# Retention and two MLPs on one core: when out-product operands are begun, which banks they fill, and where loads and weight conversions stand

## The chip, the core and the metric

The kernel runs on one core of a Trainium2 chip. TensorE (PE) multiplies matrices into PSUM banks of 128 x 512 fp32, VectorE (DVE), ScalarE (ACT) and GpSimd (POOL) work element by element, each on its own queue in order, and SyncE (SP) issues the DMAs. Times are device microseconds of one launch.

## The reference

```python
for t in range(S):                                  # 4 batches, 8 heads, 768 steps, head size 64
    state = gamma * state + outer(k[:, :, t], v[:, :, t])
    y[:, :, t] = scale * q[:, :, t] @ state
x = y as rows of 512                                # 3072 rows
h = np.maximum(x @ w_in, 0.0)                       # 512 x 2048
x = h * h @ w_out                                   # 2048 x 512
xn = x / np.sqrt(np.mean(x * x, axis=-1, keepdims=True) + 1e-06) * rms_g
g = xn @ w_gate                                     # 512 x 1536
out = (g * (1 / (1 + np.exp(-g))) * (xn @ w_val)) @ w_out2   # 1536 x 512
```

## The kernel before

**Numbers.** Every large product is made of three: an operand is cut into a high part (a cast to fp32r, by ACT) and a low part (source minus high, by DVE), and high x high, high x low and low x high are summed in a bank (`mm3`). The weights arrive as 64-bit floats. `convert` makes fp32 of them: one ACT operation (`magnitude`, L146) and two integer operations on DVE (L151, L152) per step of 128 x 512. A **tick** (`tick`) finishes step i-1, starts the magnitude of i+1 and converts i; `fetch` asks SP for the raw weight three steps ahead. W1 has 32 steps, W2 36. A finished W2 step is written back to DRAM (`finish2`, wq and wp); magnitudes have three buffers (tile f), so the magnitude of a tick takes the buffer whose write the tick before issued.

**Stages.** The tokens are six blocks of 512 (four chunks of 128, one of each batch). The recurrence is done by chunks: scores of queries and keys times a decay table (tile Pt, DVE), times values, plus queries times state. All but the first four chunks are done in **visits** between the products of the block before: `into_state` (keys times values), `values`, `scores` of the next chunk.

1. *Lead-in* (0 to 22.46 us): chunks 0 to 3, first weights.
2. *Block 0* and *block 1* (to about 258 us): `block1`. A step f is 12 products with w_in (`proj`, bank ph[f % 2]), Relu and square, and 12 products with w_out of the step before (`out1`, banks pa, pb). Block 0 converts W1; in block 1 `factory` combines pieces of w_out into seven operand tables per quarter (Winograd's form of a 2 x 2 product, P1 to P7).
3. Blocks 2, 3 as the *first pair*, 4, 5 as the *second*. *In-phase* (`in_phase`): steps f of two projections, t = 0, 1, Relu and square into tiles act. *Out-phase* (`out_phase`): 28 units of 12 products, seven products of four units each, with differences of act as operands. P2, P5 and P3 are summed in pr, P1, P6, P7 and P4 in ph; after four units the sum is copied (`take`, ACT) or added (`add`, DVE). `operand(n + ahead)` makes a whole operand: difference (DVE, L97), cast (ACT, L93), low part (DVE, L90). W2 is converted in both in-phases. The second in-phase also loads the sums of blocks 0 and 1 (yn) and their scales (rr) and prepares second-MLP operands from them (`prep_x`); the second out-phase makes its first weight units (`make_unit`).
4. *Second MLP* (from 657.39 us): three pairs of blocks, each of twelve turns of `pair`: seven products of 12, and 24 products with the last weight.

The norm (`rsqrt`) sums squares with a product against ones, then takes root, reciprocal and one Newton step in pieces that `background` calls one at a time.

**Order.** The program is written out by hand: on each queue the instructions stand as the Python code issues them, and each waits for its operands in that place.

Of the kernel before, what the change touches and what calls it, by code (L numbers as in the profile page):

```python
# [38 lines left out]
PREP_IN = 8  # L39

# [11 lines left out]
def retention_then_two_mlps(  # L52
# [85 lines left out]
    def fetch(i):  # L138
        if i < upto[0] and i not in loads:
            loads[i] = wp.tile([128, 512, 2], I32, tag="w", name="raw")  # L140
            nc.sync.dma_start(loads[i].rearrange("p n t -> p (n t)"), steps[i][2].bitcast(I32))
# [6 lines left out]
    def convert(i):  # L148
# [7 lines left out]
        fetch(i + 3)  # L156

    def tick(low_first=False):
# [5 lines left out]
        if i < upto[0]:  # L164
            magnitude(i)
            magnitude(i + 1)
# [8 lines left out]
    def more_steps(n):  # L175
        upto[0] = min(upto[0] + n, len(steps))
        for i in range(at[0], at[0] + 3):
            fetch(i)
# [27 lines left out]
    def proj(w, x, h):  # L206
        xh, xl = x[0], x[1]
        for k in range(KC):
            wc = slice(k * 128, (k + 1) * 128)
            mm3(h, w[:, 0, wc], w[:, 1, wc], xh[k], xl[k], k == 0, k == KC - 1)  # L210
# [38 lines left out]

    def rsqrt(js, sqs, last=False):  # L250
# [5 lines left out]
        m = tp.tile([128, n, 2 * C], F32, tag="y", name="m")  # L256
        for i in range(n):
            nc.vector.tensor_scalar(m[:, i], tots[0][i], 1.0 / DM, EPS, op0=ALU.mult, op1=ALU.add)
        r = tp.tile([128, n, 2 * C], F32, tag="y", name="rr")
# [9 lines left out]
        for i, j in enumerate(js):  # L269
            nc.sync.dma_start(rrs[j].rearrange("(a b) t -> a (b t)", a=2), r[0:128:D, i, :])  # L270
# [60 lines left out]
    NOUT = 7 * NQ  # L331
    prepared = {}

    def operand(n, pairs):
        if n >= NOUT or n in prepared:
            return
        k, q = divmod(n, NQ)
# [9 lines left out]
        prepared[n] = pairs(n)  # L347
        split(*prepared[n], {P2: x10, P1: x00, P5: x00, P6: x00, P7: x01, P3: x11, P4: x10}[k], nc.vector)

    def out_phase(s, pairs, ahead, y_tile, extra):  # L350
# [8 lines left out]

        for n in range(NOUT):  # L360
            k, q = divmod(n, NQ)
            acc = pr if k in (P2, P5, P3) else ph
            u = units(next_unit())
            xh, xl = prepared.pop(n)
            for m in range(2):
                mc = slice(m * 128, (m + 1) * 128)
                for c in range(2):
                    mm3(
                        acc[m], u[:, c, 0, mc], u[:, c, 1, mc], xh[:, c], xl[:, c],
                        k in (P2, P1, P5) and q == 0 and c == 0, q == NQ - 1 and c == 1, skip_group_check=True,  # L370
                    )
            unit_done()
            if q == NQ - 1:
# [8 lines left out]
            operand(n + ahead, pairs)  # L382
            extra(n, y)
        return y
# [165 lines left out]
    with tc.manual_schedule():  # L550
# [13 lines left out]
        def put(c, qq, k_, vv, kk, *more):  # L564
            nc.sync.dma_start(qq, qT[c])
            nc.sync.dma_start(k_, kT[c])
            for m in more:
                nc.sync.dma_start(*m)
            nc.sync.dma_start(vv, vn[c])
            chunk[c] = (qq, k_, vv, kk)  # L570

        def load(c):
            if c < NCH:
# [6 lines left out]
                for t, src in zip(chunk[c][2:], (vn, kn)):  # L580
                    nc.sync.dma_start(t, src[c])
# [11 lines left out]
        def stage(c, *more):  # L593

            t = [slot(f"stage{c}{i}") for i in range(2)]
            qq, k_ = (t[0][:, i, :].rearrange("p (a i) -> p a i", a=NP) for i in range(2))
            vv, kk = (t[1][:, i, :].rearrange("p (a h d) -> p a h d", a=NP, h=2) for i in range(2))
            put(c, qq, k_, vv, kk, *more)
# [79 lines left out]
        def visit(c, next_banks, with_sums):  # L678
            kv = into_state(c)
            if with_sums:  # L680
                sums([pr[0][:, 2 * C:]])
# [12 lines left out]
        stage(0, *((decays[:, h], dec[:, h]) for h in range(2)))  # L694
        for t, src in ((vdec_sb, vdec), (sdec_sb, sdec), (tri_sb, tri)):
            nc.scalar.dma_start(t, src)
        fetch(0)
        for c in range(1, CB):
            stage(c)
        fetch(1)  # L700
# [9 lines left out]
        keep_warm(WARM)  # L710
        nc.sync.dma_start(chunk[0][3], kn[0])
        fetch(2)
# [4 lines left out]
        cur = Operand(True)  # L717

        def early_values(c, bank):
            values(c, [bank.rearrange("p (a i) -> p a i", a=NP)])  # L720
            cur.put(columns_of(c), [bank.rearrange("p (a i) -> p a i", a=NP)])

        scores(0, pa, early=True)
        keep_warm(WARM // 2)
        magnitude(0)
        convert(0)
        scores(1, pb, early=True)
        early_values(0, pr[1])
        low0 = finish1(w1_keys[0], done.pop(0))
        decay_v(0, nc.scalar)  # L730
        scores(2, pa, early=True)
        low0()
        early_values(1, pr[0])
        scores(3, pb, early=True)
        early_values(2, ph[0])
        early_values(3, ph[1])
        magnitude(1)
        convert(1)
        magnitude(2)
        at[0] = 2  # L740
        for c in range(1, CB):
            nc.sync.dma_start(chunk[c][3], kn[c])
        nc.sync.dma_start(g_sb, rmsg)

        def first_states(f):

            for c, n in enumerate((0, 2, 6, 10)):
                if f == n:
                    take_state(c, into_state(c))
            if f == 0:  # L750
                load(CB + 1)
                load_q(CB + 1)
            if f == 1:
# [420 lines left out]
```

## Time and profile before

| | |
|---|---|
| median of 3 runs | 1219.46 us (1215.66 to 1223.73) |
| profiled execution | 1216.87 us, span 1215.0 us |
| busy: PE, PE weight loads | 1155.6 us (95%), 934.2 us (77%) |
| busy: DVE, ACT, POOL | 743.0 us (61%), 593.7 us (49%), 44.4 us (4%) |
| mean granted TensorE clock | 0.985 |
| DMA | 175.46 MB, 144 GB/s |

A busy PE is not a PE at its pace: a product of 512 columns is shown as about 392 ns, but the next one starts after 227 ns, so delays below that difference show nowhere as idle. A stage is therefore also read as its length against its number of products. "Idle before" is put down to what came last.

### The profile page before, as it was taken

The numbers are of one execution on the slowest core, as the hardware profiler recorded it, in microseconds if no ns is written. First come the engines' busy times: TensorE is split into PE (matmuls) and PEld (weight loads), VectorE is DVE, ScalarE is ACT, GpSimd is POOL, SyncE is SP. The second block draws the span as 40 slices with busy tenths as digits, with TensorE's granted clock in tenths as the row PEclk, the third lists the DMA queues.
The fourth block names the chain that finished last, engine by engine and source line by source line (L and its number), as shares of the span: only waits on it lengthen the run. The fifth ranks groups of instructions, "written<-read, shape, count | busy, mean of one in ns | idle before, by whom it ended". The sixth has DMA issues, their size and how long they took to land.

```text
span 1215.0 us, 15870 instructions
## 1 busy us (share of the span) xinstructions
PE 1155.6 (95%) x6070; PEld 934.2 (77%) x6070; DVE 743.0 (61%) x1090; ACT 593.7 (49%) x1071; POOL 44.4 (4%) x39
## 2 busy tenths in 40 slices
PE   7899999899999899799897899999999999999998
PEld 6688887678887688577675688888888888888887
DVE  5777346733525665444666777876777766777740
ACT  4788545355544336555245455443554443454431
POOL 0000121112110000000000000000000000000000
PEclk9899999999999999899999999999999999999999
DMA  9662436677893469983551031122111131211001
GB/s 356 232 224 83 139 122 231 220 258 271 259 338 126 170 208 342 344 283 121 181 182 67 30 96 53 44 90 88 54 56 35 44 121 62 70 35 44 27 1 70
DMA packets 74212, 175.46 MB, mean 144 GB/s; under 512 B 7948, under 2 KB 20632, under 8 KB 73880
## 3 DMA queue, kind: packets, MB, share of 16 engines
q1 hardware_dynamic: 73560, 174.24, 41.1%
q8 instruction: 48, 0.79, 0.3%
q10 hardware_dynamic: 576, 0.20, 0.1%
q14 instruction: 28, 0.23, 0.1%
HBM read 129.31 MB, written 45.10 MB: 144 GB/s over the span
## 4 chain that ended last, share of the span: by engine, by line
PE 77%; DVE 10%; ACT 7%; issue 3%; DMA 3%; SPq 0%; ACTq 0%; DVEq 0%
PE ph L181 13%; PE ph L182 12%; PE ph L183 12%; PE pr L181 7%; PE pr L182 7%; PE pr L183 7%; DVE act L97 2%; PE pa L181 2%; PE pa L182 2%; PE pa L183 2%; PE pb L181 2%; PE pb L183 2%; PE pb L182 2%; ACT o L93 2%; DMA wq<-f 1%
## 5 line engine op out<-in xcount | busy, mean ns | idle before, releaser
L181 PE MATMUL ph<-xop,ring 128*128 128x512 f32 x288 | 113.5, 394 | 6.0 <-DVE part L100 5.8
L182 PE MATMUL ph<-xop,ring 128*128 128x512 f32 x288 | 112.6, 391 | 0.0
L183 PE MATMUL ph<-xop,ring 128*128 128x512 f32 x288 | 112.6, 391 | 0.0
L181 PE MATMUL ph<-xh,w_i 128*128 128x512 f32 x256 | 102.0, 398 | 5.7 <-DVE Pt L626 5.0
L182 PE MATMUL ph<-xl,w_i 128*128 128x512 f32 x256 | 100.4, 392 | 0.2 <-DVE xl L90 0.2
L183 PE MATMUL ph<-xh,w_i 128*128 128x512 f32 x256 | 100.3, 392 | 0.0
L181 PE MATMUL pr<-xop,ring 128*128 128x512 f32 x216 | 85.0, 393 | 1.4 <-DVE part L100 1.3
L182 PE MATMUL pr<-xop,ring 128*128 128x512 f32 x216 | 84.8, 393 | 0.0
L183 PE MATMUL pr<-xop,ring 128*128 128x512 f32 x216 | 84.6, 392 | 0.0
L90 DVE TENSOR_TENSOR o<-act,o 128x1024 fp32r<-128x1024 f32 x38 | 45.9, 1223 | 52.8 <-ACT o L93 52.8
L90 DVE TENSOR_TENSOR ring<-q,ring 128x512 fp32r<-128x512 f32 x90 | 57.4, 686 | 32.0 <-ACT ring L93 32.0
L93 ACT CAST o<-act 128x1024 fp32r<-128x1024 f32 x38 | 39.1, 1049 | 63.0 <-DVE act L97 60.0
L181 PEld LDWEIGHTS ph<-xop,ring 128*128 128x128 f32 x288 | 54.4, 189 | 20.1 <-DVE part L100 6.2
L183 PEld LDWEIGHTS ph<-xop,ring 128*128 128x128 f32 x288 | 54.4, 189 | 11.4
L182 PEld LDWEIGHTS ph<-xop,ring 128*128 128x128 f32 x288 | 54.4, 189 | 11.1
L181 PEld LDWEIGHTS ph<-xh,w_i 128*128 128x128 f32 x256 | 48.4, 189 | 18.4 <-DVE Pt L626 6.7
L327 ACT ACTIVATE act<-ph 128x512 f32<-128x512 f32 x64 | 38.0, 594 | 49.0 <-PE ph L183 48.5
L181 PE MATMUL ph<-xh,ring 128*128 128x512 f32 x128 | 51.0, 398 | 10.0 <-ACT act L327 10.0
L146 ACT ACTIVATE f<-raw 128x512 f32<-128x512 f32 x68 | 45.4, 669 | 29.9 <-DMA wq<-f 16.0
L480 ACT ACTIVATE t<-part 128x512 f32<-128x512 f32 x54 | 34.2, 633 | 45.9 <-DVE part L100 44.6
L183 PEld LDWEIGHTS ph<-xh,w_i 128*128 128x128 f32 x256 | 48.4, 189 | 10.7 <-DVE w_i L90 0.4
L182 PEld LDWEIGHTS ph<-xl,w_i 128*128 128x128 f32 x256 | 48.5, 189 | 10.3 <-DVE xl L90 0.5
(227 smaller groups left out, 2774.7 us busy)
## 6 DMA issues: line engine op xcount, KB each, us to landing
ring<-uo SPq DMA_DIRECT2D x56, 512.0 KB, 3.3
q<-wq SPq DMA_DIRECT2D x72, 256.0 KB, 3.2
raw<-w1i SPq DMA_DIRECT2D x16, 512.0 KB, 7.5
raw<-w1o SPq DMA_DIRECT2D x16, 512.0 KB, 7.0
uo<-made SPq DMA_DIRECT2D x16, 512.0 KB, 2.6
wi<-w_i SPq DMA_DIRECT2D x16, 512.0 KB, 6.5
ring<-wi SPq DMA_DIRECT2D x16, 512.0 KB, 4.6
uo<-w_o SPq DMA_DIRECT2D x24, 256.0 KB, 5.2
```

Of the source, the lines that this page charges most:

```text
L90: eng.tensor_tensor(out=dst_l, in0=src, in1=dst_h.bitcast(F32), op=ALU.subtract)
L93: nc.scalar.copy(dst_h, src)
L97: nc.vector.tensor_tensor(out=out_, in0=a, in1=b, op=ALU.subtract)
L146: nc.scalar.activation(sizes[i], loads[i].bitcast(F32)[:, :, 1], AF.Prelu, scale=REBIAS, alpha=NEGATIVE)
L181: nc.tensor.matmul(acc, ah, bh, start=start, stop=False, **more)
L182: nc.tensor.matmul(acc, ah, bl, start=False, stop=False, **more)
L183: nc.tensor.matmul(acc, al, bh, start=False, stop=stop, **more)
L327: nc.scalar.activation(a, ph[t], AF.Relu)
L480: nc.scalar.activation(t, g, AF.Sigmoid)
```

## The change

- **Out-phases.** `operand` becomes `operand_hi` (difference and cast, for unit n + ahead + 1) and `operand_lo` (low part, for unit n + ahead), called in this order. The units run in the order SEQ; P5 and P3 are summed in pa.
- **Lead-in.** Loads stand by need: queries, keys and tables of the chunks before values and the first weight; the early scores and values are called alternately; the first projection runs its high products first. Raw weights are fetched five steps ahead, up to step 24.
- **Block 0.** Values are decayed by DVE instead of ACT and at other steps; chunk 0's state product moves from step 0 to 2, chunk 1's from 2 to 4; the first scores there use ph[1] and pr[0].
- **Block 1.** The combining (three calls of `made` a step) moves from before the visit to after it. W2 conversions begin at step 10.
- **W2.** 6, 18 and 12 steps in block 1, first and second in-phase; before 0, 14 and 22. Ticks of the first in-phase: each t = 0, and t = 1 at f = 3, 7, 11; of the second: t = 0, and t = 1 at 6 and 11 (before both t). yn and rr are loaded after f = 5, before after f = 4.
- **Norm.** Sums in 32 partitions a chunk and 128 columns a block (before 64 and 256); the last norm waits four calls before its root.

```diff
-        fetch(i + 3)
+        fetch_to(i + AHEAD if i + AHEAD < EARLY else max(i + 3, EARLY - 1))
...
     def sums(tot):
         if due:
             tots, sqs = due.pop(0)
+            tot = tot[:, :len(sqs) * C].rearrange("p (n i) -> p n i", i=C)
             tots.append(tot)
             for i, sq in enumerate(sqs):
-                for h in range(2):
-                    for c in range(2):
-                        n = 2 * c + h
-                        nc.tensor.matmul(
-                            tot[i][c * D:(c + 1) * D, h * C:(h + 1) * C], ones, sq[:, n * C:(n + 1) * C],
-                            start=True, stop=True,
-                        )
+                for c in range(CB):
+                    nc.tensor.matmul(
+                        tot[c * PQ:(c + 1) * PQ, i], ones[:, :PQ], sq[:, c * C:(c + 1) * C], start=True, stop=True
+                    )
...
+        nc.vector.tensor_scalar(m, tots[0], 1.0 / DM, EPS, op0=ALU.mult, op1=ALU.add)
+        for _ in range(last):
+            yield
...
+    SEQ = [(k, q) for k in (P2, P1) for q in range(NQ)]
+    SEQ += [(P5, 0), (P5, 1), (P6, 0), (P5, 2), (P6, 1), (P5, 3), (P6, 2), (P6, 3), (P3, 0), (P3, 1)]
+    SEQ += [(P7, q) for q in range(NQ)] + [(P3, 2), (P3, 3)] + [(P4, q) for q in range(NQ)]
...
-        prepared[n] = pairs(n)
-        split(*prepared[n], {P2: x10, P1: x00, P5: x00, P6: x00, P7: x01, P3: x11, P4: x10}[k], nc.vector)
+        src = {P2: x10, P1: x00, P5: x00, P6: x00, P7: x01, P3: x11, P4: x10}[k]
+        h, l = pairs(n)
+        nc.scalar.copy(h, src)
+        begun[n] = (h, l, src)
+
+    def operand_lo(n):
+        if n in begun:
+            h, l, src = begun.pop(n)
+            low(nc.vector, l, src, h)
+            prepared[n] = h, l
...
-            acc = pr if k in (P2, P5, P3) else ph
+            acc = {P2: pr, P1: ph, P5: pa, P6: ph, P7: ph, P3: pa, P4: ph}[k]
...
-            operand(n + ahead, pairs)
+            operand_hi(n + ahead + 1, pairs)
+            operand_lo(n + ahead)
             extra(n, y)
...
+        stage_in(0, "q", "k")
+        for h in range(2):
+            nc.sync.dma_start(decays[:, h], dec[:, h])
...
+        stage_in(1, "q", "k")
+        stage_in(0, "v")
+        stage_in(2, "q", "k")
+        stage_in(1, "v")
+        stage_in(3, "q", "k")
+        fetch_to(0)
...
-            for c, n in enumerate((0, 2, 6, 10)):
+            for c, n in enumerate((2, 4, 6, 10)):
                 if f == n:
                     take_state(c, into_state(c))
...
+                decay_v(0, nc.vector)
+                decay_v(CB, nc.vector)
...
-                    scores(at_chunk, pr)
+                    scores(at_chunk, (ph[1], pr[0]))
...
+        def early1(f):
+            if f == MORE_AT:
+                more_steps(W2_FIRST)
+            if f > MORE_AT:
+                tick()
+
+        def last1(f):
             if f >= 5:
                 for _ in range(3):
                     next(made, None)
...
-            if t == 0 and 1 <= f:
+            if t == 0 or f % 4 == 3 and f < 12:
                 tick()
...
-            if 1 <= f <= 11:
+            if 1 <= f <= 11 and (t == 0 or f in (6, 11)):
                 tick()
...
-            if f == 4 and t == 1:
+            if f == 5 and t == 1:
```

How it moves instructions, at three places. SP in the lead-in, before (stage_178, 190, 195 hold queries and keys of chunks 0 to 2, stage_179, 191 the values of 0 and 1, raw a weight of twice the size):

```order
L565 DMA stage_178<-qT 128x512
L566 DMA stage_178<-kT 128x512
L568 DMA decays<-dec 128x512 x2
L569 DMA stage_179<-vn 128x512
L141 DMA raw<-w1i 128x1024
L565 DMA stage_190<-qT 128x512
L566 DMA stage_190<-kT 128x512
L569 DMA stage_191<-vn 128x512
L565 DMA stage_195<-qT 128x512
```

and now (178, 180, 182, 184 queries and keys, 179, 181 values):

```order
L625 DMA stage_178<-qT 128x512
L625 DMA stage_178<-kT 128x512
L725 DMA decays<-dec 128x512 x2
L625 DMA stage_180<-qT 128x512
L625 DMA stage_180<-kT 128x512
L625 DMA stage_179<-vn 128x512
L625 DMA stage_182<-qT 128x512
L625 DMA stage_182<-kT 128x512
L625 DMA stage_181<-vn 128x512
L625 DMA stage_184<-qT 128x512
L625 DMA stage_184<-kT 128x512
L150 DMA raw<-w1i 128x1024
```

The second chunk's keys move from the ninth tile to the sixth, the weight behind the fourth chunk's keys.

DVE in the second out-phase at P5 and P6, before (act the operands' sources, o their low parts):

```order
L97 TENSOR_TENSOR act_4169<-act_4196,act_4169 128x1024
L90 TENSOR_TENSOR o<-act_4169,o 128x1024
L97 TENSOR_TENSOR act_4373<-act_4399,act_4373 128x1024
L90 TENSOR_TENSOR o<-act_4373,o 128x1024
L97 TENSOR_TENSOR act_4562<-act_4577,act_4562 128x1024
L90 TENSOR_TENSOR o<-act_4562,o 128x1024
```

and now:

```order
L102 TENSOR_TENSOR act_4337<-act_4356,act_4337 128x1024
L95 TENSOR_TENSOR o<-act_3979,o 128x1024
L102 TENSOR_TENSOR act_4154<-act_4269,act_4154 128x1024
L95 TENSOR_TENSOR o<-act_4337,o 128x1024
L102 TENSOR_TENSOR act_4498<-act_4513,act_4498 128x1024
L95 TENSOR_TENSOR o<-act_4154,o 128x1024
```

Each low part stood right behind its own difference; now another operand's difference stands between.

SP in the second in-phase around the loads of yn, before (wq, wp the writes of converted steps, ring the next w_in):

```order
L985 DMA yn_4200<-ys_72 128x2048
L985 DMA yn_4202<-ys_73 128x2048
L393 DMA rr<-rrs_78 128x512
L393 DMA rr<-rrs_79 128x512
L129 DMA wq_131<-f 128x2x256
L141 DMA raw<-w2v 128x1024
L129 DMA wq_131<-f 128x2x256
L141 DMA raw<-w2o 128x1024
L307 DMA ring_3354<-wi_96 128x1024
```

and now:

```order
L1040 DMA yn_4214<-ys_72 128x2048
L1040 DMA yn_4216<-ys_73 128x2048
L422 DMA rr<-rrs_78 128x512
L422 DMA rr<-rrs_79 128x512
L134 DMA wq_132<-f 128x2x256
L150 DMA raw<-w2o 128x1024
L132 DMA wp_143<-f 128x512
L150 DMA raw<-w2g 128x1024
L320 DMA ring_3357<-wi_97 128x1024
```

Both times two steps' writes and raw loads follow the loads before the next w_in does.

## Rows read from the trace of the kernel before

**Rows 1.** Stretches: length, busy PE PEld DVE ACT POOL (count), clock, DMA share, GB/s.
```profile
0.00:22.46 22.46, 15.68 (x158) 13.05 (x158) 9.06 (x17) 6.87 (x17) 0.20 (x4) 0.92 0.95 342
22.46:140.00 117.54, 113.28 (x790) 90.90 (x791) 79.00 (x140) 90.35 (x219) 1.04 (x1) 0.97 0.51 182
140.00:258.00 118.00, 112.98 (x836) 90.75 (x835) 65.07 (x110) 54.16 (x113) 22.77 (x18) 0.99 0.55 194
258.00:371.30 113.30, 112.21 (x826) 90.64 (x824) 40.95 (x73) 61.45 (x118) 20.41 (x16) 1.00 0.79 275
371.30:457.67 86.37, 80.69 (x336) 64.59 (x337) 53.44 (x49) 30.00 (x33) 0.00 (x0) 0.96 0.54 182
457.67:558.28 100.61, 90.59 (x401) 73.82 (x400) 47.12 (x69) 60.21 (x95) 0.00 (x0) 0.97 0.83 299
558.28:657.39 99.11, 84.49 (x337) 62.61 (x336) 67.16 (x64) 42.05 (x48) 0.00 (x0) 0.98 0.43 146
...
711.41:735.90 24.49, 24.49 (x108) 20.01 (x107) 19.35 (x32) 12.77 (x23) 0.00 (x0) 1.00 0.20 65
```

**Rows 2.** TensorE's waits over the span: who, releaser, us in total, times, longest.
```profile
PE ph L181 <- ACT act L327: 10.0, 2, 8.3
...
PE ph L181 <- DVE part L100: 5.8, 1, 5.8
PE ph L181 <- DVE Pt L626: 5.0, 4, 2.3
...
PE ph L181 <- ACT y L104: 3.5, 1, 3.5
```

**Rows 3.** Sum of the seven stretches with TensorE's clock at 0.50.
```profile
sum 34.10, PE 27.02 PEld 20.92 DVE 25.57 ACT 18.67 POOL 0.00; mean PE 3.86 PEld 2.99 DVE 3.65 ACT 2.67 POOL 0.00
```

**Rows 4.** Timeline of TensorE, 4 to 47 us: start, length, instruction, count, [idle before].
```profile
11.48 2.08 PE L623 MATMUL pb<-stage 64*128 64x128 f32 x16 [3.98 <-DMA stage<-kT]
...
22.46 0.50 PE L181 MATMUL ph<-xh,w_i 128*128 128x512 f32 x1 [0.69 <-ACT xh L93]
...
38.20 1.72 PE L623 MATMUL pr<-qnt,kTt 64*128 64x128 f32 x16 [2.61 <-DVE qnt L602]
41.29 1.12 PE L636 MATMUL pr<-stage 128*64 128x64 f32 x16 [1.37 <-DVE Pt L626]
```

**Rows 5.** Timeline of DVE in block 0: a decay of one chunk's queries.
```profile
37.46 0.69 DVE L602 TENSOR_TENSOR qnt<-qnt,qdec_sb 128x512 f32<-128x512 f32 x1
```

**Rows 6.** Groups of instructions, page: count, busy us, mean ns, idle before, releaser.
```profile
L146 ACT ACTIVATE f<-raw 128x512 f32<-128x512 f32 x68 | 45.4, 669 | 29.9 <-DMA wq<-f 16.0
```

**Rows 7.** DMA issues, 258 to 370 us: count, KB each, median us to landing.
```profile
wq<-f SPq DMA_DIRECT2D x10, 256.0 KB, 6.0
```

**Rows 8.** Chain of waits in the second out-phase: start, us, what.
```profile
587.49 1.23 DVE o L90
588.71 1.15 DVE act L97
...
589.96 1.06 ACT o L93
```

**Rows 9.** Timeline of SP and ACT in the second in-phase.
```profile
488.22 0.90 SPq L985 DMA_DIRECT2D yn<-ys  x2
...
490.32 0.44 SPq L129 DMA_DIRECT2D wq<-f  x1
...
501.57 0.66 ACT L146 ACTIVATE f<-raw 128x512 f32<-128x512 f32 x1 [10.51 <-DMA wq<-f]
```

**Rows 10.** Timeline of DVE in the second MLP's first pair.
```profile
678.98 3.35 DVE L264 RECIPROCAL rr<-rr 128x512 f32<-128x512 f32 x1
```

**Rows 11.** Timeline of ACT there: the second table load and what follows.
```profile
668.91 1.28 ACT L262 ACT_TABLE_LOAD   x1
670.20 0.23 ACT L262 ACTIVATE scratch<-ones 128x32 f32<-128x32 f32 x1
```

**Rows 12.** Timeline of ACT one pair later, at the place that receives the root.
```profile
709.83 0.62 ACT L93 CAST ring<-mix 128x512 fp32r<-128x512 f32 x1 [2.04 <-DVE mix L97]
```

More of the change, by code (lines that the diff above doesn't have):

```diff
@@ L39 @@
 PREP_IN = 8
+AHEAD = 5
+EARLY = 24
+MORE_AT = 10
+W2_FIRST = 6
+W2_NEXT = 18
 P2, P1, P5, P6, P7, P3, P4 = range(7)
@@ L136, in retention_then_two_mlps, with fetch_to @@
     at, upto = [0], [n1_steps]
-    def fetch(i):
-        if i < upto[0] and i not in loads:
+    fetched = [0]
+    def fetch_to(n):
+        while fetched[0] <= min(n, upto[0] - 1):
+            i = fetched[0]
+            fetched[0] += 1
             loads[i] = wp.tile([128, 512, 2], I32, tag="w", name="raw")
@@ L155, in convert, with tick @@
         done[i] = f
-        fetch(i + 3)
-    def tick(low_first=False):
+        fetch_to(i + AHEAD if i + AHEAD < EARLY else max(i + 3, EARLY - 1))
+    def tick(low_first=False, ahead=True):
         i = at[0]
@@ L165, in tick @@
             magnitude(i)
-            magnitude(i + 1)
+            if ahead:
+                magnitude(i + 1)
         if low_first and rest_of:
@@ L176, in more_steps @@
         upto[0] = min(upto[0] + n, len(steps))
-        for i in range(at[0], at[0] + 3):
-            fetch(i)
+        fetch_to(at[0] + 2)
     def mm3(acc, ah, al, bh, bl, start, stop, **more):
@@ L204, in put, with proj @@
                 split(h, l, src, nc.vector)
[L206 to L210, printed above, removed]
+    def proj(w, x, h, highs_first=False):
+        parts = ((0, 0), (0, 1), (1, 0))
+        if highs_first:
+            order = [(a, b, k) for a, b in parts for k in range(KC)]
+        else:
+            order = [(a, b, k) for k in range(KC) for a, b in parts]
+        for n, (a, b, k) in enumerate(order):
+            nc.tensor.matmul(
+                h, w[:, a, k * 128:(k + 1) * 128], x[b][k], start=n == 0, stop=n == len(order) - 1
+            )
     back = []
@@ L255, in rsqrt @@
         n = len(js)
[L256 to L259, printed above, removed]
+        m = tp.tile([128, n, C], F32, tag="y", name="m")
+        nc.vector.tensor_scalar(m, tots[0], 1.0 / DM, EPS, op0=ALU.mult, op1=ALU.add)
+        for _ in range(last):
+            yield
+        r = tp.tile([128, n, C], F32, tag="y", name="rr")
         nc.scalar.activation(r, m, AF.Sqrt)
@@ L579, in load, with load_v @@
                 ]
-                for t, src in zip(chunk[c][2:], (vn, kn)):
-                    nc.sync.dma_start(t, src[c])
+                if c > CB:
+                    load_v(c)
+        def load_v(c):
+            for t, src in zip(chunk[c][2:], (vn, kn)):
+                nc.sync.dma_start(t, src[c])
         def load_q(c):
@@ L591, in load_k, with stage, stage_in @@
                 nc.sync.dma_start(chunk[c][1], kT[c])
-        def stage(c, *more):
+        def stage(c):
             t = [slot(f"stage{c}{i}") for i in range(2)]
-            qq, k_ = (t[0][:, i, :].rearrange("p (a i) -> p a i", a=NP) for i in range(2))
-            vv, kk = (t[1][:, i, :].rearrange("p (a h d) -> p a h d", a=NP, h=2) for i in range(2))
-            put(c, qq, k_, vv, kk, *more)
+            chunk[c] = [t[0][:, i, :].rearrange("p (a i) -> p a i", a=NP) for i in range(2)]
+            chunk[c] += [t[1][:, i, :].rearrange("p (a h d) -> p a h d", a=NP, h=2) for i in range(2)]
+        def stage_in(c, *which):
+            for w in which:
+                nc.sync.dma_start(chunk[c]["qkv".index(w)], {"q": qT, "k": kT, "v": vn}[w][c])
         def decay_q(c, eng):
@@ L710, in retention_then_two_mlps, with early_values @@
         keep_warm(WARM)
+        fetch_to(2)
         nc.sync.dma_start(chunk[0][3], kn[0])
-        fetch(2)
+        fetch_to(AHEAD - 1)
+        cur = Operand(True)
+        def early_values(c, bank):
+            values(c, [bank.rearrange("p (a i) -> p a i", a=NP)])
+            return lambda: cur.put(columns_of(c), [bank.rearrange("p (a i) -> p a i", a=NP)])
+        scores(0, pa, early=True)
+        keep_warm(WARM // 2)
+        scores(1, pb, early=True)
+        early_values(0, pr[1])()
+        scores(2, pa, early=True)
+        early_values(1, pr[0])()
+        scores(3, pb, early=True)
+        put2 = early_values(2, ph[0])
         nc.sync.dma_start(qdec_sb, qdec)
@@ L716, in retention_then_two_mlps @@
         load_k(CB)
[L717 to L724, printed above, removed]
         magnitude(0)
         convert(0)
-        scores(1, pb, early=True)
-        early_values(0, pr[1])
+        put2()
         low0 = finish1(w1_keys[0], done.pop(0))
-        decay_v(0, nc.scalar)
-        scores(2, pa, early=True)
+        early_values(3, ph[1])()
         low0()
[L733 to L736, printed above, removed]
         magnitude(1)
         convert(1)
+        load_v(CB)
         magnitude(2)
         at[0] = 2
-        for c in range(1, CB):
-            nc.sync.dma_start(chunk[c][3], kn[c])
-        nc.sync.dma_start(g_sb, rmsg)
         def first_states(f):
-            for c, n in enumerate((0, 2, 6, 10)):
+            for c, n in enumerate((2, 4, 6, 10)):
                 if f == n:
@@ L774, in tail1, with block1 @@
                 next(back[-1])
-        def block1(j, x, sink, visit_at, early, late):
+        def block1(j, x, sink, visit_at, early, late, last_of=lambda f: None):
             nonlocal prev, at_chunk
@@ L1045, in retention_then_two_mlps @@
         fold(y2, 0)
-        back.append(rsqrt([NB - 2, NB - 1], [y2[1][t][:, 0] for t in range(2)], last=True))
+        back.append(rsqrt([NB - 2, NB - 1], [y2[1][t][:, 0] for t in range(2)], last=4))
         next(back[-1])
```

113 lines of the change are left out of this document (62 added, 51 removed).

## The prediction

> **What bounds the kernel now.** I read the busy times by stage first, then TensorE's waits, then the timeline at each wait. In pair 1 of the second MLP TensorE issues 108 products in 24.49 us and never waits: 0.2268 us a product, 2.72 us for a unit of twelve, is its pace [rows 1]. The change alters neither number nor size of the large products, so only TensorE's idle time and its time at the lower clock can be won. The waits show who holds it: ACT's Relu, DVE's adds and low parts, ACT's copy of a finished bank [rows 2]. After longer waits the granted clock stands at 0.50, the 1.2 GHz level: seven stretches, 34.10 us in all, in which half is lost, 17 us [rows 3]. A wait that goes thus often gives back more than itself. The reader should hold each stage against this pace: the first pair's out-phase takes 86.37 us for 336 products that need 76.2, a loss of 10.2; the second pair's 99.11 for 337 (76.4), a loss of 22.7; the first pair's in-phase waits nowhere [rows 1, 2].
>
> **The sum, stage by stage.**
>
> *Lead-in.* The second chunk's scores waited 3.98 us for its keys, and the first projection started at 22.46 [rows 4]. Those keys were the ninth tile of 262 KB on SP's queue (the first weight counts as two) and are now the sixth; at 342 GB/s a tile takes 0.77 us [rows 1], so they land 2.3 us earlier. That is the low end. The first weight's two integer operations and its low part leave the DVE queue ahead of the scores; at 0.69 us each, the row of a DVE operation of the same width [rows 5], 2.1 us more. The high end is all idle time of the stretch, 22.46 - 15.68 = 6.8. I take 4.4, the two reasons together. High products first cost nothing: same twelve products.
>
> *Block 0.* At its third step TensorE waited 2.61 for the decayed queries and 1.37 for the score bank [rows 4], then ran 6.8 us at 0.50, another 3.4 [rows 3]: 7.4. Decay is now queued earlier, and the scores take one bank of another pair, so both go. What is late next is chunk 0's state product: the decay of its values sits on DVE behind two conversions, where ACT had done it before the projection ended. I put 1.5 us on that, two DVE operations [rows 5]; nothing is the low price, the old 4.0 the high one. Five raw weights ahead cost SP slots, not TensorE time; ACT loses its decays, DVE gains nine of about 0.69 inside 79 of 117.5 busy [rows 1, 5]. Net 5.9, lead-in and block together 10 (4 to 14).
>
> *Block 1.* The scores wait behind DVE's weight-combining work, 5.0 us in four waits [rows 2], with one low-clock stretch (1.7). The combining now stands after the visit and just ahead of the out product, so DVE meets the scores first. Six W2 conversions come in: per step 0.67 of ACT [rows 6] and two DVE operations (at most 0.69 each), 8 us of DVE where 53 of 118 are free [rows 1]. I take 5.5 of the 6.7 (2 to 6.7).
>
> *First in-phase.* 18 conversions instead of 14; each loads 0.52 MB and writes 0.26, 3.1 MB on top of 275 GB/s x 113.3 us = 31 MB, DMA share 0.79 to 0.87 [rows 1]. Three ticks now follow another by one projection. ACT's next magnitude needs the buffer whose write was issued one tick earlier, and such a write takes 6.0 us [rows 7]; ACT is late there, but each of the three falls on a visit, which gives TensorE other work. I take a loss of 0.5 (6 to nothing).
>
> *First out-phase.* Its loss of 10.2 is a chain, not load: difference on DVE 1.15, cast on ACT 1.06, low part on DVE 1.23 [rows 8], one after the other, 3.5 us a unit against 2.72. With the next difference queued ahead of the low part, the cast runs beside it, and a unit costs DVE 1.15 + 1.23 = 2.4, under the pace. The bank handover after P6 (3.5 [rows 2]) is now covered by two units of P3, 5.4 us; with it goes the low clock behind it. First-unit waits of 1.2 stay: 9 gained (7 to 10.2).
>
> *Second in-phase.* Its loss is 10.0 of waits for ACT's Relu [rows 2] and 3.4 of clock. Rows 9 show the longest: SP issues the two loads of the normalised blocks' inputs at 488.22, the weight write at 490.32 queues behind them, and ACT's magnitude waits for that write until 501.57, the Relu behind it. Fewer conversions suggest that this goes, but the change moves both: the loads are issued after step 5, the only early double tick is at step 6, directly behind them. The same write again stands behind the same 2.6 MB, and ACT now has a cast of the normalised input in front of the Relu too, about 1 us. Less other traffic saves about as much. I keep the long wait at 7.5 to 8 with its clock, let the short one of 1.7 go and gain 2 (-2 to 13.4).
>
> *Second out-phase.* The same chain goes, but DVE is busy 67 us [rows 1] of what would be 76. Two places stay late. At the start six DVE operations of the input preparation, each low waiting for its own cast, hold the third to fifth operand: 4.5. In the last seven units two adds, four differences, low parts and the weight units (0.69 an operation of half width [rows 5]) make 17 us of DVE for 13.6 of products: 3.9. With 0.3 between, 8.7 of 22.7 stay: 14 gained (9 to 20).
>
> *Second MLP.* The reciprocal of 3.35 us [rows 10] and its three followers of 0.69 stand before the add that TensorE waits 5.8 for [rows 2]; one low-clock stretch (1.7) follows. In 128 columns they halve, 2.8 us in all, and come two pairs later, where I leave 1.0; 0.4 stays here. The square root moves to pair 1, two table loads of 1.28 [rows 11], 0.35 and 0.23, 3.1 us of ACT where it idled 2.04 [rows 12]; the 1.1 left over lies in front of an add with that much slack. 6 gained (3 to 7.5). The rows show no time lost around a load: the load of 668.91 ends when the next instruction starts, at 670.20 [rows 11]. The Trainium skill speaks against this move: ScalarE: Activation LUTs, section What ACT_TABLE_LOAD costs, puts a drain of about 1.38 us on each switch besides the load. By that, an estimate, the move would cost TensorE about 2 us and the sum would be 2 higher; I stay with the rows.
>
> Sum: 10 + 5.5 - 0.5 + 9 + 2 + 14 + 6 = 46. The profiled execution took 1216.9 (span 1215.0), 2.6 under the median of 1219.46 and inside the runs' 1215.66 to 1223.73; 1216.9 - 46 gives 1171.
>
> **Rivals.**
> 1. *The second in-phase runs through.* Five conversions instead of eight stand ahead of the loads, the queue is empty then, and the write lands in time: another 7.5 and 3.4 of clock, 1160. For it: less traffic; against: the write is issued behind the loads all the same. Chance 0.18.
> 2. *DVE stays the bound of the second out-phase and of block 0's start.* At 67 of 76 us every wait for a cast pushes it over the pace; half of the 14 and 4 us of block 0 are lost: 1182. Chance 0.17.
> 3. *Moved conversions stall ACT in parts.* The three double ticks and the shared buffer in block 1 wait as in rows 9, three to four waits of 3 us with clock: 1186. Chance 0.05.
> 4. *Slower: the first in-phase becomes paced by writes.* Should each write there take 11.3 us (490.32 to 501.57 [rows 9]) instead of 6.0, ACT would wait 11.3 - 5.45 (two projections, the distance of ticks) - 2.7 (the Relu's slack) = 3.1 us at each of 18 ticks, 56 us, and every such idle has 1.7 of low clock behind it, 31 us: 1258. It decides from a write time of about 8.2 us; the sum above is eaten at 2.6 us a tick. Against it: 0.87 is still below a full queue. Chance 0.04.
> 5. *The change does not do what it says*, its banks or orders waiting on each other elsewhere: within 1%, chance 0.03.
>
> **How the numbers follow.** The forecast has 0.53. A difference below 1%, 12 us, can't be told from none. Only rivals 4 and 5 end above 1207: faster 0.93, same 0.03, slower 0.04. For the range: the low end takes rival 1 with a little more, 1157; the high end takes rivals 2 and 3, 1187; about 1 in 6 is outside. The bounds of all terms at their low ends together, 1195, are not to be expected.
>
> **What would show it.** Right: differences and low parts on DVE back to back in the out-phases, units 2.72 us apart except at the start and the last seven units of the second; first projection near 18; no 5.8 wait in pair 0; the second in-phase's long wait at step 7 on ACT's Relu, released by a write. Wrong: magnitudes that wait for writes in the first in-phase, score waits in block 1, an out-phase above 3 us a unit, or a square root in pair 1 followed by a TensorE gap.

## The result, and the profile after

The change takes 1190.82 us (median of four runs, 1188.92 to 1191.54), the kernel before on the same chip 1218.88 (1215.66 to 1223.73): ratio 0.9764, 95% interval 0.9729 to 0.9799. It is faster, by 28 us where 46 were forecast, and 1191 lies outside the range of 1157 to 1187. The profiled execution took 1190.94, span 1189.2.

The stretches of the change, cut at the first product of each stage (columns as in [rows 1]; lead-in, block 0, block 1, first in-phase, first out-phase, second in-phase, second out-phase, second MLP):

```profile
0.00:18.26 18.26, 13.75 (x158) 11.54 (x159) 8.52 (x16) 5.03 (x8) 0.20 (x4) 1.00 0.91 321
18.26:123.68 105.42, 103.45 (x708) 83.12 (x709) 81.81 (x146) 73.89 (x150) 1.04 (x1) 1.00 0.59 215
123.68:261.70 138.02, 125.43 (x929) 101.20 (x928) 73.95 (x125) 61.05 (x127) 23.82 (x18) 0.96 0.57 200
261.70:373.88 112.18, 109.52 (x813) 88.15 (x811) 45.14 (x81) 62.71 (x121) 20.34 (x16) 1.00 0.86 310
373.88:450.18 76.30, 76.30 (x336) 63.20 (x337) 53.00 (x49) 30.23 (x33) 0.00 (x0) 1.00 0.62 204
450.18:548.05 97.87, 90.11 (x401) 73.28 (x400) 33.65 (x48) 54.07 (x85) 0.00 (x0) 0.97 0.69 228
548.05:635.26 87.21, 80.19 (x337) 63.59 (x336) 64.67 (x63) 40.53 (x46) 0.00 (x0) 0.98 0.48 163
635.26:1189.20 553.94, 542.52 (x2393) 445.20 (x2391) 380.16 (x574) 249.98 (x433) 0.00 (x0) 1.00 0.17 58
```

[Rows 1] cut block 1 roughly. Cut in the same way, from its first projection to the in-phase's second, it took in the kernel before:

```profile
132.74:261.28 128.54, 123.34 (x929) 98.82 (x928) 68.18 (x114) 59.03 (x126) 22.77 (x18) 0.99 0.53 187
```

| stage | before | change | gained | forecast |
|---|---|---|---|---|
| lead-in and block 0 | 132.74 | 123.68 | 9.1 | 10 |
| block 1 | 128.54 | 138.02 | **-9.5** | **5.5** |
| first in-phase | 110.02 | 112.18 | -2.2 | -0.5 |
| first out-phase | 86.37 | 76.30 | 10.1 | 9 |
| second in-phase | 100.61 | 97.87 | 2.7 | 2 |
| second out-phase | 99.11 | 87.21 | 11.9 | 14 |
| second MLP | 557.61 | 553.94 | 3.7 | 6 |
| sum | 1215.0 | 1189.2 | 25.8 | 46 |

Fifteen of the twenty missing microseconds are in one row, block 1: forecast 5.5 shorter, it is 9.5 longer at a mean clock of 0.96. TensorE's costliest waits, and the sum of its four stretches at a granted clock of 0.50 (223.25, 257.39, 496.32 and 564.59 us; in answer to [rows 2, 3]):

```profile
PE ph L222 <- ACT act L340: 9.5, 3, 7.7
PE ph L650 <- issue: 9.5, 4, 6.2
PE ph L191 <- DVE o L95: 5.1, 4, 2.6
PE ph L190 <- DVE t L511: 3.1, 3, 1.5
PE pa L190 <- ACT s L238: 2.9, 1, 2.9
```

```profile
sum 20.48, PE 15.83 PEld 12.74 DVE 13.99 ACT 10.97 POOL 2.73; mean PE 3.96 PEld 3.19 DVE 3.50 ACT 2.74 POOL 0.68
```

DVE's wait of 5.8 and ACT's handover of 3.5 are gone, and so are the four waits of projections on Pt, which reads the score bank. New are the second and the fifth row, both in block 1; the fourth, in the second MLP, has grown from 0.2. Two of these waits in TensorE's timeline there (L650 are the scores of a visit, L190 an out product):

```profile
224.20 2.08 PE L650 MATMUL ph<-qnt,kTt 64*128 64x128 f32 x16 [6.20 <-issue]
...
256.87 0.50 PE L190 MATMUL pa<-s,w_o 128*128 128x512 f32 x1 [2.88 <-ACT s L238]
```

"issue" says that the trace shows no releaser. ACT's timeline at the first one does (L155 the W2 magnitude, L235 the Relu that frees the score bank, L98 a cast of the combining):

```profile
215.79 0.62 ACT L98 CAST made<-sm 128x512 fp32r<-128x512 f32 x1 [2.83 <-DMA qnt<-qT]
222.96 0.66 ACT L155 ACTIVATE f<-raw 128x512 f32<-128x512 f32 x1 [6.56 <-DMA wq<-f]
223.52 0.58 ACT L235 ACTIVATE r<-ph 128x512 f32<-128x512 f32 x1
```

The Relu ends at 224.10 and the scores start at 224.20. It had stood behind a magnitude that waited 6.56 for the write-back of its buffer. SP issued that write at 218.30, behind a store of the combining whose low part DVE ended at 217.90:

```profile
217.93 0.33 SPq L884 DMA_DIRECT2D uo<-made  x1
218.30 0.43 SPq L134 DMA_DIRECT2D wq<-f  x1
```

At the second wait it is the same: a magnitude waits 4.57 for a write until 254.36, and the Relu and the cast of s stand behind it. So the theory is: block 1 lost its 15 us because a W2 magnitude waits there for one of three buffers, the Relu waits behind it, and the scores behind the Relu, with half clock after each long wait. The rival blames the moved combining, whose casts now stand on ACT between a visit and the next Relu.

### The profile page after: what moved, and what is told of

Read it like the earlier page. It is cut to its first block, busy times and chain, and to the rows that moved or that the text cites. A ratio compares the mean times of both kernels' runs of the same rounds, so it can differ in the third digit from the quotient of the medians.

```text
span 1189.2 us, 15789 instructions
## 1 busy us (share of the span) xinstructions
PE 1141.3 (96%) x6070; PEld 929.3 (78%) x6070; DVE 740.9 (62%) x1097; ACT 577.5 (49%) x999; POOL 45.4 (4%) x39
## 4 chain that ended last, share of the span: by engine, by line
PE 80%; DVE 7%; DMA 6%; ACT 4%; issue 2%; SPq 1%; ACTq 0%; DVEq 0%
PE ph L222 18%; PE ph L190 7%; PE ph L191 7%; PE ph L192 7%; PE pr L190 7%; PE pr L191 7%; PE pr L192 7%; PE pa L190 3%; PE pa L191 3%; PE pa L192 3%; PE pb L190 2%; PE pb L192 2%; PE pb L191 2%; PE pr L674 2%; DMA wq<-f 1%
## 5 line engine op out<-in xcount | busy, mean ns | idle before, releaser
L222 PE MATMUL ph<-xh,w_i 128*128 128x512 f32 x512 | 165.4, 392 | 2.8 <-ACT act L340 1.7
L190 PE MATMUL ph<-xop,ring 128*128 128x512 f32 x288 | 113.0, 392 | 4.3 <-DVE t L511 3.1
L222 PE MATMUL ph<-xh,ring 128*128 128x512 f32 x256 | 81.1, 396 | 7.8 <-ACT act L340 7.7
L190 PE MATMUL pr<-xop,ring 128*128 128x512 f32 x216 | 84.5, 391 | 1.9 <-DVE part L105 1.8
L190 PEld LDWEIGHTS ph<-xop,ring 128*128 128x128 f32 x288 | 54.0, 188 | 18.4 <-DVE t L511 5.7
L222 PEld LDWEIGHTS ph<-xh,ring 128*128 128x128 f32 x256 | 48.8, 191 | 19.3 <-ACT act L340 8.8
L155 ACT ACTIVATE f<-raw 128x512 f32<-128x512 f32 x68 | 45.0, 667 | 34.3 <-DMA wq<-f 24.2
L109 ACT COPY part<-ph 128x512 f32<-128x512 f32 x76 | 43.1, 586 | 17.9 <-PE ph L192 17.9
```

The costliest lines, as they stand in the source:

```text
L109: nc.scalar.copy(dst[:, m], acc[m])
L155: nc.scalar.activation(sizes[i], loads[i].bitcast(F32)[:, :, 1], AF.Prelu, scale=REBIAS, alpha=NEGATIVE)
L190: nc.tensor.matmul(acc, ah, bh, start=start, stop=False, **more)
L222: nc.tensor.matmul(h, w[:, a, k * 128:(k + 1) * 128], x[b][k], start=n == 0, stop=n == len(order) - 1)
```

## The experiments

All compute the full result. Experiments 1, 3, 6 to 9 and 11 were run once, and every stage length is that of one profiled execution; the second MLP, which 1 to 9 leave as it is, took 553.8 to 556.1 in the change and these nine. In the first four expectations "block 1" counts from its third projection to the in-phase's second, 14.3 us shorter than the rows here (114.2 for 128.5, 123.7 for 138.0).

**1. Block 1 without W2 conversions.**

```diff
-W2_FIRST = 6
+W2_FIRST = 0
```

> The six W2 conversions leave block 1; they are done in the second in-phase instead (eighteen there, five of them in one go at step 12), so only the part up to the first out-phase's end is read from this run. Block 1, from its first projection to the first product of the in-phase, took 114.2 us in the kernel before and 123.7 in the change. Theory (ACT comes late to the Relu that the scores wait for, because a W2 magnitude ahead of it waits for the write-back of its buffer): the waits of 6.2 and 2.9 us and the two half-clock stretches of 6.8 and 3.4 behind them (5.1 lost) go, about 14 us: block 1 near 110. Rival (the combining's casts, now queued between the visit and the next Relu, make ACT late): the 6.2 wait may shrink, but waits of 1 to 2 us at the scores stay at most visits, block 1 above 117.

**2. The combining before the visit.**

```diff
-        block1(1, ..., early1, keep_out, last1)
+        def late1(f):
+            keep_out(f)
+            last1(f)
+
+        block1(1, ..., early1, late1)
```

> The combining of W1's output weights stands ahead of the visit again, as in the kernel before; the six W2 conversions stay in block 1. Theory (write-backs of the W2 buffers): block 1 stays at 120 to 126 us, the whole 1188 to 1194. Rival (the casts of the combining ahead of the Relu): block 1 falls to 111 to 115, the whole to 1180 to 1184.

**3. Both.**

> Both edits of block 1 undone together, read up to the in-phase. If these two hold the whole difference, block 1 is at 114 us again, the kernel before's 114.2. Against the run without W2 conversions alone it prices the moved combining by itself: my forecast's reason (DVE meets the scores first) says that the moved one is 4 to 6 us faster, the rival that it is 3 or more slower.

**4. One more buffer.**

```diff
-        cf = ... tc.tile_pool(name="cf", bufs=3)
+        cf = ... tc.tile_pool(name="cf", bufs=4)
```

> One more buffer for the W2 magnitudes (four instead of three, 2 KB a partition), nothing else. Theory (waits for write-backs of those buffers): in block 1 the magnitudes find a free buffer, 6.2 and 2.9 us of waits with the clock behind them go, block 1 near 111 instead of 123.7; in the second in-phase the wait of 7.75 at step 7 with 3.4 of clock goes too, 97.9 to about 87 to 90; the whole near 1168. Rival (the queue itself is late, so that the fourth buffer only puts the wait one conversion later; or the cast of the normalised input, which waits for its 1 MB loads, holds ACT in the same place): block 1 above 118 and the second in-phase above 95, the whole 1183 to 1192.

Block 1, first without W2 conversions, then with the combining before the visit, with both, and with four buffers:

```profile
123.08:246.37 123.29, 120.55 (x930) 97.98 (x929) 69.06 (x113) 56.34 (x118) 22.79 (x18) 1.00 0.53 187
```

```profile
122.94:261.24 138.30, 127.12 (x929) 101.30 (x928) 74.27 (x125) 61.18 (x127) 23.54 (x18) 0.95 0.60 206
```

```profile
123.06:250.54 127.48, 121.97 (x930) 97.53 (x928) 68.55 (x115) 57.75 (x121) 24.03 (x18) 1.00 0.54 188
```

```profile
122.80:247.52 124.72, 122.10 (x930) 99.13 (x928) 73.22 (x123) 59.92 (x125) 24.16 (x18) 0.99 0.63 219
```

The conversions cost 138.02 - 123.29 = 14.7 us; with the combining in its old place 138.30 - 127.48 = 10.8. The moved combining by itself is 127.48 - 123.29 = 4.2 faster, as forecast; beside the conversions it is worth nothing (138.30 against 138.02, the whole 1189.07). With a fourth buffer the same six conversions cost 124.72 - 123.29 = 1.4. The rival falls as the main cause: its casts leave two waits of 0.7 and 1.9. The missing buffer is the cause of nearly all, and the whole kernel takes 1179.50 (1177.25 to 1179.85), ratio 0.9689 [0.9666, 0.9712] to the kernel before. Whether the write, issued ahead of the combining's store, would have freed the third buffer in time was not tried.

The other half of the expectation failed: the second in-phase stayed at 97.8. In the change, where the loads of yn were issued at 484.61, SP and ACT had shown this there:

```profile
486.69 1.08 SPq L134 DMA_DIRECT2D wq<-f  x1
...
497.67 0.67 ACT L155 ACTIVATE f<-raw 128x512 f32<-128x512 f32 x1 [9.74 <-DMA wq<-f]
```

With four buffers ACT and DVE show this (L98 the cast of the normalised input, L429 the normalising):

```profile
484.19 1.05 ACT L98 CAST xop<-yn 128x1024 fp32r<-128x1024 f32 x1 [8.95 <-DVE yn L429]
```

```profile
482.74 1.42 DVE L429 SCALAR_TENSOR_TENSOR yn<-yn,g_sb,rr 128x512 f32<-128x512 f32 x2 [14.47 <-DMA rr<-rrs]
```

Another instruction, in the same place, waits for the same loads.

**5. Four buffers, preparation two steps later; 6. the latter with three buffers.**

```diff
-                if f >= 6 and next(prep_count) < PREP_IN:
+                if f >= 8 and next(prep_count) < PREP_IN:
```

> The fourth buffer for the W2 magnitudes as before, and the preparation of the normalised input starts at step 8 of the second in-phase instead of step 6. With four buffers alone TensorE still waited 6.96 us there, and ACT's line now names the cast of the normalised input, 8.95 us idle, released by DVE's normalising, which waits for the 2.6 MB of loads. Theory (two things stand in front of the Relu, one behind the other: first the write-back, then that cast): the wait goes, the second in-phase falls from 97.8 to 88.5 to 90, the whole from 1179.5 to about 1171. Rival (the queue behind those loads is itself the limit, so that the next tile of w_in or the next raw weight holds TensorE or ACT instead): the second in-phase stays above 95, the whole above 1177.

> Three buffers as in the change, only the preparation of the normalised input begins at step 8 instead of step 6. Theory: the write-back alone holds ACT in the same place and as long, the second in-phase stays at 95 to 98.7 and block 1 at about 124 us (third projection to the in-phase). Rival (the cast alone held it): the second in-phase 88 to 90.

The second in-phase took 95.07 and 96.43 us. ACT's wait there with four buffers, and with three:

```profile
486.37 0.66 ACT L155 ACTIVATE f<-raw 128x512 f32<-128x512 f32 x1 [7.71 <-DMA raw<-w2o]
```

```profile
494.68 0.66 ACT L155 ACTIVATE f<-raw 128x512 f32<-128x512 f32 x1 [8.49 <-DMA wq<-f]
```

Theory 5 fell: the wait shrank to 4.77 on TensorE, but now a raw weight releases it. A write-back, a cast and a raw weight stand in a row, and each is late for the same 2.6 MB of loads: the cast waits for them, the two transfers are queued behind them. That one reason is still a theory here; experiment 9 tests it. The whole is 1175.68 (1173.94 to 1177.16), ratio 0.9640 [0.9612, 0.9668].

**7. Cast and difference with their low part; 8. the old order and banks.**

```diff
-            operand_hi(n + ahead + 1, pairs)
+            operand_hi(n + ahead, pairs)
             operand_lo(n + ahead)
```

```diff
-    SEQ = [(k, q) for k in (P2, P1) ...
+    SEQ = [(k, q) for k in range(7) for q in range(NQ)]
...
-            acc = {P2: pr, P1: ph, P5: pa, P6: ph, P7: ph, P3: pa, P4: ph}[k]
+            acc = pr if k in (P2, P5, P3) else ph
```

> The operands of the out-phases are no longer begun one step ahead: difference, cast and low part of one operand are queued together, as in the kernel before; order and banks of the change stay. Theory (the chain of 3.5 us a unit against a pace of 2.72 is what the early start removes, and the order only the handover of a bank): the first out-phase goes from 76.3 to 78 to 80, the second, where DVE has other work, from 87.2 to 94 to 99. Rival (order and banks did it): both stay within 1 us.

> Order and banks of the products in the out-phases as in the kernel before, operands still begun one step ahead. Theory (the handover of the bank after P6 cost 3.5 us with half clock behind it): the first out-phase 81 to 84 instead of 76.3, the second 91 to 95 instead of 87.2. Rival (the early start of the operands did all): both stay within 1 us of the change.

First and second out-phase without the early start, and with the old order:

```profile
373.82:457.49 83.67, 79.10 (x337) 62.48 (x337) 53.37 (x49) 29.97 (x33) 0.00 (x0) 1.00 0.57 189
553.79:653.54 99.75, 84.71 (x337) 62.72 (x336) 66.96 (x64) 40.53 (x46) 0.00 (x0) 0.98 0.43 144
```

```profile
372.49:448.78 76.29, 76.29 (x336) 63.17 (x337) 52.59 (x49) 30.34 (x33) 0.00 (x0) 1.00 0.64 205
547.88:630.67 82.79, 77.98 (x337) 62.61 (x336) 64.08 (x62) 40.47 (x46) 0.00 (x0) 1.00 0.52 172
```

The early start does nearly all of it: without it the second out-phase is as long as before the change (99.75 against 99.11), the first 2.7 shorter than before (83.67 against 86.37); both are longer than I had expected. The old order loses nothing in the first (76.29) and is 4.4 shorter in the second: 1.7 of that is half clock that comes or goes (below), and the waits of 0.52 and 1.71 near the end are missing. My expectation for the old order was wrong: in the kernel before, the handover of 3.5 came from ACT's copy of the bank, which started only at 421.73, behind a cast that had waited for DVE:

```profile
420.78 1.04 ACT L93 CAST oh<-act 128x1024 fp32r<-128x1024 f32 x1 [2.50 <-DVE act L97]
421.73 1.06 ACT L104 COPY y<-ph 128x512 f32<-128x512 f32 x2
```

With the early start the casts don't wait so, and the copies start with the bank, in either order.

**9. The loads apart** (on four buffers and the later preparation).

```diff
-            if f == 5 and t == 1:
-                for t_ in range(2):
-                    yn.append(big(f"yn{t_}"))
-                    nc.sync.dma_start(yn[t_], ys[t_])
+            if f in (1, 5) and t == 1:
+                t_ = len(yn)
+                yn.append(big(f"yn{t_}"))
+                nc.sync.dma_start(yn[t_], ys[t_])
+            if f == 6 and t == 1:
                 prep[0] = prep_x(...)
```

> Four buffers, preparation from step 8, and the two 1 MB loads of the normalised blocks' inputs apart: one after step 1, one after step 5, the scales after step 6. With both together TensorE waited 4.77 us although neither write-back nor cast stood there: ACT's magnitude waited 7.71 for a raw weight issued behind the loads. Theory (whatever stands on the queue behind 2.6 MB at once comes late, and ACT meets one of it before the Relu): the long wait goes, the second in-phase falls from 95.1 to 89 to 91. Rival (the stage moves more than the queue carries, so that the wait only comes elsewhere in it): above 93.5.

The second in-phase fell to 91.40, just above the 89 to 91 expected, TensorE's long wait to 2.19; the whole took 1172.62 in its one run. So the burst on the queue made most of the wait, not the amount of data, which is the same. What is left is again a raw weight, behind the second load and the double tick of step 6.

**10. The old order, and the last norm in pieces (on the edits of 5); 11. the root back in pair 0 (on the change).**

```diff
-        nc.vector.reciprocal(r, r)
-        yield
+        pieces = [slice(i, i + 1) for i in range(n)] if last else [slice(0, n)]
+        for a in pieces:
+            nc.vector.reciprocal(r[:, a], r[:, a])
+            yield
...
```

```diff
-        for _ in range(last):
+        for _ in range(0):
             yield
```

> Four buffers, preparation from step 8, order and banks of the out-phases as in the kernel before, and the reciprocal and its three followers by halves, one piece in each of pairs 2 to 5 instead of all in pair 2. Theory for the out-phases (the new order costs 2 to 4 us in the second, where two adds and the low parts come late): 82.8 to 84.4 instead of 86.9. Theory for the MLP (3 us of DVE in one pair hold its add, 1.2, and the next handover, 1.5): these two waits of 710 and 717 us fall to below 0.5 each, the second MLP 2 us shorter. Rival: the 1.5 is the handover of a bank that the pairs before show as well (0.5 and 1.1), and stays. The whole 1175.7 less 4 to 6: 1170 to 1172.

> The change, with the square root and what follows it back in the second MLP's pair 0, in 128 columns as in the change: it prices the move alone. Theory (the narrower tile did half, the move the rest): the wait of 5.8 us of the kernel before comes back as 2.5 to 3.5 in pair 0, the waits of 1.1, 1.2 and 1.5 in pairs 1 and 2 go, so that the second MLP stands within 1.5 us of the change's 553.9. Rival (the move did it, a table load in pair 0 holds DVE's add as before): 2 or more longer, with half clock behind the wait.

TensorE's waits in pairs 1 and 2 of the change, and in pair 0 with the root there:

```profile
690.67 0.50 PE L190 MATMUL ph<-xop,ring 128*128 128x512 f32 x1 [1.10 <-DVE t L511]
711.22 0.50 PE L190 MATMUL ph<-xop,ring 128*128 128x512 f32 x1 [1.19 <-DVE part L105]
718.50 0.50 PE L190 MATMUL ph<-xop,ring 128*128 128x512 f32 x1 [1.48 <-DVE t L511]
```

```profile
661.58 0.49 PE L190 MATMUL ph<-xop,ring 128*128 128x512 f32 x1 [1.74 <-DVE part L105]
668.80 0.50 PE L190 MATMUL ph<-xop,ring 128*128 128x512 f32 x1 [1.47 <-DVE t L511]
```

In pieces, the 1.2 goes and the 1.5 falls to 0.8, but 0.8 to 0.9 comes in pairs 3 and 4 as well: 553.33 for the second MLP, no gain that shows. With the root in pair 0 it is 555.41, of which 3.4 is lost in a half-clock stretch ahead of the root (642.3 to 649) that most kernels with the change's MLP have too: these took 553.8 to 556.1 over the runs. In pair 0 the narrower tile has turned the wait of 5.8 into 1.7 and 1.5, about as much as the change's pieces together (1.1, 1.2 and 1.5); the move gained nothing that can be told. The old order, here with four buffers and the later preparation, gave 84.34 for the second out-phase, the whole 1171.47 (1171.07 to 1171.71), ratio 0.9611 [0.9595, 0.9627].

**12. Together.**

```diff
-W2_FIRST = 6
-W2_NEXT = 18
+W2_FIRST = 24
+W2_NEXT = 0
...
-            if 1 <= f <= 11 and (t == 0 or f in (6, 11)):
+            if 1 <= f <= 11 and (t == 0 or f in (9, 11)):
```

with the edits of 4, 5, 8, 9 and 11.

> What the runs point to, together: four buffers, preparation from step 8, the loads of the normalised inputs apart, order and banks of the out-phases as in the kernel before, the root in pair 0 again, the second double tick of the second in-phase at step 9 instead of 6, and the raw loads of the first in-phase's W2 steps begun from block 1 on, since its first wait (2.05 to 2.5 us) was released by a raw weight whose load is issued at the in-phase's start. Theory (each stage's wait has its own cause, so that the gains add): from the spread loads' 1172.6, 2.5 from the order, 2 from the last wait of the second in-phase, 2 to 2.5 from the first in-phase, 1 from the root: 1164 to 1167. Rival (the moved ticks and earlier loads meet other transfers in block 1 and the second in-phase): 1169 to 1173, with a new wait on ACT's Relu or the scores in one of them.

Median 1164.08 (1163.37 to 1164.47), ratio to the kernel before 0.9560 [0.9538, 0.9582]. Block 1, first in-phase, second in-phase and second out-phase:

```profile
125.25:248.71 123.46, 120.88 (x929) 97.89 (x928) 73.24 (x123) 59.39 (x124) 23.53 (x18) 1.00 0.65 225
248.71:358.83 110.12, 109.20 (x814) 88.16 (x812) 46.19 (x82) 63.71 (x123) 20.45 (x16) 1.00 0.87 315
...
435.12:523.80 88.68, 88.20 (x401) 72.31 (x400) 33.83 (x48) 54.10 (x85) 0.00 (x0) 1.00 0.74 252
523.80:606.61 82.81, 78.03 (x338) 62.60 (x337) 64.33 (x63) 40.72 (x46) 0.00 (x0) 1.00 0.52 172
```

The gains add up, with the same 18 conversions in the first in-phase: its loss of 2.2 was the raw weights of its first step, whose loads the change issues only at its start (the first at 265.80), so that ACT waits there:

```profile
271.96 0.66 ACT L155 ACTIVATE f<-raw 128x512 f32<-128x512 f32 x1 [5.12 <-DMA raw<-w2g]
```

In both in-phases no wait on ACT's Relu above 0.5 is left. Only the root in pair 0 paid nothing: TensorE waits 2.8 for it there, and the second MLP takes 555.4.

## Why the forecast was too high

- **Lead-in and block 0: right, with a term that the sum did not have.** First projection at 18.26, forecast "near 18": 4.2 gained for 4.4, in block 0 4.9 for 5.9. But the lead-in's mean clock was 0.92 before and is 1.00 now: a half-clock stretch there (about 11.3 to 14.7 us) that [rows 3] leave out is gone, and how much of the 4.2 it made no run tells. In block 0 both waits and the half clock behind them are gone, and chunk 0's state product waits 0.6 for the decay, as foreseen; a wait of 1.3 for a Relu was not.
- **Block 1: the failed step.** "DVE meets the scores first" was right in effect (4.2 of the 5.5 when nothing else is added), though what waited before was the projection behind the scores, for Pt to read their bank, and not the scores ([rows 2], L181). The step priced the six conversions as 8 us of DVE work that fits into idle time. It gave ACT 0.67 a step and did not ask what ACT waits for, although the in-phase term two lines on does: the magnitude needs a buffer that a write frees, there are three, and the combining holds one of them. Nor did it ask who is queued behind: the Relu, and at each visit the scores that need its bank at once. Rival 3 named this shared buffer at 0.05; its 15 us were the right size.
- **First in-phase: mis-sized**, 0.5 against 2.2, and by another cause than the write-backs named: the first raw weights come late. Rival 4 did not occur.
- **First out-phase: right in size (10.1 for 9), half wrong in cause.** The early start alone gives all of it; the handover was a part of the same chain, and with it the new order covers nothing.
- **Second in-phase: right** (2.7 for 2). The long wait stayed, at step 7, on ACT's Relu, released by a write. That removing the write would not have freed it, since a cast and a raw weight are as late, was not seen.
- **Second out-phase: mis-sized by 2.1.** The first three waits, 4.3 us, are the 4.5 forecast; half clock behind them cost 1.7 more. The waits at the end are 2.5 for the 3.9 forecast, 2.2 of them the new order's, not DVE's load: the old order has the same adds and low parts. The other 2.3 of the loss of 10.8 show nowhere as idle.
- **Second MLP: mis-sized, 3.7 for 6.** The 5.8 went, but as pieces: waits of 7.7 us stand where 8.3 stood (0.2, 1.0, 1.3 and 5.8). What makes the 3.7 are two half-clock stretches of 3.4 us behind the old waits, 1.7 lost in each; the sum had one of them. That the change's trace has none was luck, as far as the others tell: of the nine other traces with the same second MLP (experiments 1 to 9) eight have 3.4 or 6.8 us of it, 8 to 11 us after the stage's start, and take 554.4 to 556.1, which is 1.5 to 3.2 less than before. "The 1.1 left over lies in front of an add with that much slack" failed: the cast behind the root starts at 680.80, DVE idles 1.79 for it, and TensorE waits 1.1 in that pair.
- **Two sums that do not come out.** The low ends of the terms add to 17 gained, which is 1200 and not 1195; and 17 us of DVE less 13.6 of products is 3.4, not 3.9. Neither moves the forecast by more than 0.5.

ACT and DVE at the square root of the second MLP:

```profile
677.65 1.28 ACT L273 ACT_TABLE_LOAD   x1
678.94 0.42 ACT L273 ACTIVATE rr<-m 128x256 f32<-128x256 f32 x1
...
680.80 0.60 ACT L98 CAST ring<-mix 128x512 fp32r<-128x512 f32 x1
```

```profile
681.43 0.69 DVE L95 TENSOR_TENSOR ring<-mix,ring 128x512 fp32r<-128x512 f32 x1 [1.79 <-ACT ring L98]
```

The Trainium skill (ScalarE: Activation LUTs, section What ACT_TABLE_LOAD costs) adds a drain of about 1.38 us to each load. The trace again shows none: the load of 677.65 ends at 678.93 and the root starts at 678.94.

## What to carry to other kernels

Work that is moved onto an engine with idle time brings its waits with it: before pricing it by its duration, list what each instruction waits for (a buffer's write-back, above all) and who stands behind it on that queue. When several instructions in turn release the same wait, look for what they have in common, here one burst of loads, and spread that. And a stall that is cut into pieces of about the same sum gives back only the half clock behind it, and here that came or went between executions.

## What the runs showed of the hardware

The same waits may or may not be followed by half clock. In the second out-phase of the change and of the kernel with the combining before the visit TensorE waits 0.60, 1.12, 2.60 and 0.60, 1.10, 2.56 us; behind the third, the change and the other kernel:

```profile
564.59:568.00 3.41, 3.41 (x9) 2.63 (x8) 2.72 (x3) 2.42 (x4) 0.00 (x0) 0.50 0.00 0
```

```profile
563.09:566.50 3.41, 3.41 (x16) 2.80 (x16) 2.72 (x3) 2.55 (x4) 0.00 (x0) 1.00 0.00 0
```

That is 1.7 us between two executions of the same stage, and bounds what a single run can tell.

Some of DVE's operations take longer while POOL works. Beside two decays of POOL (216.08 to 218.80 us) two took 1.46 and 1.26 us that otherwise take 0.69 and 0.43:

```profile
216.44 1.46 DVE L95 TENSOR_TENSOR made<-sm,made 128x512 fp32r<-128x512 f32 x1 [0.69 <-ACT made L98]
217.82 1.26 DVE L160 TENSOR_SCALAR f<-f 128x512 int32<-128x512 int32 x1
```

The Trainium skill (SBUF — State Buffer, section SBUF: two separate sides) says that an operation of DVE with two SBUF inputs, or in a mode that uses two ports, and one of GpSimd take a shared pair of ports in turn, for a whole instruction. The trace agrees as far as the first of the two has two such inputs and each is longer by less than one of POOL's (1.27 and 1.49); an operation that reads a PSUM bank took its usual 0.74 beside POOL (228.99). It isn't every time: another with two such inputs, started at 196.30 beside POOL, took 0.69. In this place the first of the two put off the store and the write-back behind it by about 0.8 us.
